# Two 128x1024 blocks transposed by DMA instead of by TensorE, and one load put behind them, in an adaLN transformer block

## The chip, the cores and the metric

The kernel runs on one core of a Trainium2 chip. The metric is the device time of one execution in microseconds (us); beside it stands the span, the time from the first to the last instruction in a profiled execution.

In the text, "chunk" is 128 tokens (2048 tokens make 16 chunks), PE is TensorE, DVE is VectorE, ACT is ScalarE, POOL is GpSimd, SP is the queue that issues all DMA. A PSUM bank is a buffer that PE writes its results to; it has to be emptied ("evacuated") by DVE or ACT before it is used again. The granted clock is the share of its full clock that PE was given. "Landing" is the time at which a transfer has arrived.

## The reference, cut to what matters

```python
mod = (silu(c) @ w_mod)            # six rows of 1024: sa, ca, ga, sb, cb, gb
h = layernorm(x) * (1 + ca) + sa   # x: 2048 x 1024
q, k, v = split(h @ wqkv)          # 32 heads
# linear attention: phi(k)^T v summed over all tokens, then phi(q) times it
x = x + ga * (attention(q, k, v) @ wo)
h = layernorm(x) * (1 + cb) + sb
x = x + gb * ((gelu(h @ w_gate) * (h @ w_up)) @ w_down)
```

## The kernel before

Every chunk passes through the same steps: LN statistics on DVE, the normalized chunk "xhat" (DVE, 128 tokens x 1024), a transpose into `H1` (features on partitions), the modulation `mod1` (DVE, multiply and add in place on `H1`), and then the k, v and q matmuls. There are two ways to transpose. `t1` uses PE (eight 128x128 transposes into a PSUM bank, copied out by ACT); `t1d` is one DMA. Chunks 0 to 5 use the first, chunks 6 to 15 the second.

```python
def t1(c_, tb):                       # by PE
    b_, rng = xh_buf(c_)
    for dc in range(NDC):             # NDC = 8
        sch.op(T, lambda e, dc=dc: e.transpose(PS16(tb, dc * P, (dc + 1) * P), b_[:, dc * P:(dc + 1) * P], IDENT[:, :]), ...)
    sch.op(A, lambda e: e.activation(H1[sg][:, :, ci * P:(ci + 1) * P], PS16(tb)..., ACTF.Copy), ...)

def t1d(c_, stream=Q):                # by DMA, issued from SP
    b_, rng = xh_buf(c_)              # three buffers in rotation
    tdma(stream, H1[sg][:, :, ci * P:(ci + 1) * P], b_[:, :], ...)
...
w_dma(WV, ...); w_dma(WV, ...)        # SP queue, in this order
x_dma(4, 8)
w_dma(WQ, ..., 0, 512)
w_dma(WQ, ..., 512, 1024)
x_dma(8, 12)                          # tokens 1024 to 1535, 2 KB per token
...
for c_ in range(4):
    ...                               # two v blocks of eight matmuls each
    if c_ == 0:
        ln1(4)
        for k, t in enumerate((4, 5, 10, 11)):
            wm_dma(t, k)              # four loads of 1 MB, modulation weights
    if c_ >= 1:
        kvacc(c_ - 1)                 # phi(k)^T v of one chunk
    if c_ == 1:
        ln1(5)
    if c_ == 2:
        ln1(6)
        x_dma(12, 16)
        t1d(6)
        t1(4, 4)
        mod1(4, 1)
t1(5, 4)
mod1(5, 1)
for c_ in range(4, NCH):              # q blocks, k, v, kvacc, and ln1/t1d of chunk c_ + 3
    ...
```

A helper records the operations of each engine in the order of the program and puts in the semaphore waits. Each engine is given its own list, in that order. So where `ln1(5)` stands in the text matters only against other operations of the same engines, DVE above all.

Near 175 to 200 us, after the loop, the last twelve q blocks run, and their PSUM banks rotate.

```python
b = (0, 1, 2, 0)[qn[0]] if qn[0] < 4 else (qn[0] + 1) % 2    # bank of the next q block
...
den(0, 3); rb_load(0); rb_load(1)     # den: denominators of attention (PE); their reciprocals stored, and loaded back broadcast, by DMA
kvbd()                                # DVE
q_next(); q_next()
for u in range(NG):                   # NG = 8
    q_next()
    if u == 0:
        kvt()                         # eight PE transposes, one ACT copy
    else:
        w2_pair(u - 1)                # "W2 products": wo times a transposed kv block
    ...                               # pq_scale needs the loaded reciprocals
```

Of the kernel before, what the change touches and what calls it, by code (L numbers as in the profile page):

```python
# [214 lines left out]
def bass_adaLN_cond__linear_attn_block__geglu_ffn__prompt_kernel(  # L215
# [15 lines left out]
    with ExitStack() as es:  # L231
# [79 lines left out]
        def r_sm(name):  # L311
            return [(SMO[name], SMO[name] + SMSZ[name], name)]
# [7 lines left out]
        def r_xs(c0, c1):  # L320
            return [(OFF_XALL + c0 * D * 2, OFF_XALL + c1 * D * 2, "xall")]
# [4 lines left out]
        def r_h1(sg, k0=0, k1=NDC, s0=0, s1=SGW):  # L326
            return r_t8(H1O[sg], f"h1T{sg}", k0, k1, s0, s1)
# [54 lines left out]
        def pr(b):  # L382
            return [(b * 2048, (b + 1) * 2048)]
# [4 lines left out]
        def PS16(b, c0=0, c1=1024):  # L388
            return ps16[:, b * 1024 + c0: b * 1024 + c1]
# [41 lines left out]
        def x_dma(c0, c1):  # L431
            return sch.dma(Q, lambda e: e.dma_start(XALL[:, c0:c1, :], x_v[:, c0:c1, :]), wr=r_xs(c0, c1), note=f"x{c0}")

        def wm_dma(t, sl):
            return sch.dma(Q, lambda e: e.dma_start(WMST[sl][:], wm_v[:, :, t * 512:(t + 1) * 512]), wr=r_wm(sl), note=f"wm{t}")

        def w_dma(dst, off, name, kind, c0, c1, dc0=0, dc1=NDC):
            return sch.dma(Q, lambda e: e.dma_start(dst[:, dc0:dc1, c0:c1], wqkv_v[:, dc0:dc1, kind * D + c0:kind * D + c1]),
                           wr=[t_ for dc in range(dc0, dc1) for t_ in r_w(off, name, dc, c0, c1)], note=f"{name}.{dc0}.{c0}")
# [21 lines left out]
        x_dma(4, 8)  # L461
        w_dma(WQ, OFF_WQ, "wq", 0, 0, 512)
        w_dma(WQ, OFF_WQ, "wq", 0, 512, 1024)
        x_dma(8, 12)


        sch.op(T, lambda e: e.transpose(PS16(4, 0, NDC), C8[:, :], IDENT[0:NDC, 0:NDC]),
# [10 lines left out]
        def ln_stats(c_, tag):  # L478
            src = XALL[:, c_, :]
            sch.op(V, lambda e: e.bn_stats(STA[:, c_, 0:6], src[:, 0:512]), rd=r_x(c_), wr=r_smc("st", c_, 48), note=f"bn1 {tag}{c_}")  # L480
            sch.op(V, lambda e: e.bn_stats(STA[:, c_, 6:12], src[:, 512:1024]), rd=r_x(c_), wr=r_smc("st", c_, 48), note=f"bn2 {tag}{c_}")
            sch.op(V, lambda e: e.bn_aggr(MVA[:, c_, :], STA[:, c_, :]), rd=r_smc("st", c_, 48), wr=r_smc("mv", c_, 8), note=f"aggr {tag}{c_}")
            sch.op(V, lambda e: e.tensor_scalar(VEA[:, c_:c_ + 1], MVA[:, c_, 1:2], 1e-5, None, op0=ALU.add),
                   rd=r_smc("mv", c_, 8), wr=r_smc("ve", c_, 4), note=f"ve {tag}{c_}")
            sch.op(G, lambda e: e.tensor_tensor(RSA[:, c_:c_ + 1], VEA[:, c_:c_ + 1], NEGHALF[:, :], ALU.pow),
                   rd=r_smc("ve", c_, 4) + r_sm("neghalf"), wr=r_smc("rs", c_, 4), deps=[last_g[0]], note=f"rstd {tag}{c_}")

        def ln_nm(c_):
            sch.op(V, lambda e: e.scalar_tensor_tensor(NMA[:, c_:c_ + 1], MVA[:, c_, 0:1], -1.0, RSA[:, c_:c_ + 1],
                                                       op0=ALU.mult, op1=ALU.mult),  # L490
                   rd=r_smc("mv", c_, 8) + r_smc("rs", c_, 4), wr=r_smc("nm", c_, 4), note=f"nm {c_}")

        def xhat_dve(c_, dst, rng):
            sch.op(V, lambda e: e.tensor_scalar(dst[:, :], XALL[:, c_, :], MVA[:, c_, 0:1], RSA[:, c_:c_ + 1],
                                                op0=ALU.subtract, op1=ALU.mult),
                   rd=r_x(c_) + r_smc("mv", c_, 8) + r_smc("rs", c_, 4), wr=rng, note=f"xhat {c_}")

        def xhat_act(c_, dst, rng):
            sch.op(A, lambda e: e.activation(dst[:, :], XALL[:, c_, :], ACTF.Identity, bias=NMA[:, c_:c_ + 1], scale=RSA[:, c_:c_ + 1]),
                   rd=r_x(c_) + r_smc("nm", c_, 4) + r_smc("rs", c_, 4), wr=rng, note=f"xhata {c_}")  # L500

        def xh_buf(c_):
            i = c_ % 3
            return XH[i], r_2k(XHO[i], f"xh{i}")

        def ln1(c_, eng="dve"):
            b_, rng = xh_buf(c_)
            ln_stats(c_, "A")
            if eng == "dve":
                xhat_dve(c_, b_, rng)  # L510
            else:
                ln_nm(c_)
                xhat_act(c_, b_, rng)

        def t1(c_, tb):
            b_, rng = xh_buf(c_)
            sg, ci = divmod(c_, CPG)
            for dc in range(NDC):
                sch.op(T, lambda e, dc=dc: e.transpose(PS16(tb, dc * P, (dc + 1) * P), b_[:, dc * P:(dc + 1) * P], IDENT[:, :]),  # L519
                       rd=rng + r_sm("ident"), pwr=pr(tb), note=f"T1 {c_}.{dc}")  # L520
            sch.op(A, lambda e: e.activation(H1[sg][:, :, ci * P:(ci + 1) * P], PS16(tb).rearrange("p (a b) -> p a b", a=NDC), ACTF.Copy),
                   prd=pr(tb), wr=r_h1(sg, 0, NDC, ci * P, (ci + 1) * P), note=f"h1raw {c_}")
# [3 lines left out]
        def tdma(stream, dst, src, rng, wr_, note):  # L526
            d_ = [last_t[0]] if last_t[0] is not None and last_t[0].stream != stream else []
            last_t[0] = sch.dma(stream, lambda e: e.dma_start_transpose(out=dst, in_=src), rd=rng, wr=wr_, deps=d_, note=note)

        def t1d(c_, stream=Q):  # L530
            b_, rng = xh_buf(c_)
            sg, ci = divmod(c_, CPG)
            tdma(stream, H1[sg][:, :, ci * P:(ci + 1) * P], b_[:, :], rng, r_h1(sg, 0, NDC, ci * P, (ci + 1) * P), f"T1 {c_}")
# [73 lines left out]
        def kv_mm(c_, kind, jg, bank, dcs):  # L607
            sg, ci = divmod(c_, CPG)
            W_, off, name = (WK, OFF_WK, "wk") if kind == "k" else (WV, OFF_WV, "wv")
            o = None  # L610
            for dc in dcs:
                o = sch.op(T, lambda e, dc=dc: e.matmul(PS(bank), H1[sg][:, dc, ci * P:(ci + 1) * P], W_[:, dc, jg * 512:(jg + 1) * 512],  # L612
                                                        start=(dc == 0), stop=(dc == NDC - 1)),
                           rd=r_h1(sg, dc, dc + 1, ci * P, (ci + 1) * P) + r_w(off, name, dc, jg * 512, (jg + 1) * 512),
                           pwr=(pr(bank) if dc == 0 else ()), note=f"{kind} c{c_} jg{jg} dc{dc}")
            if dcs[-1] == NDC - 1:
                pset_writer(bank, o)
# [5 lines left out]
        def v_evac(c_, jg, bank):  # L623
            i = c_ % 3
            sch.op(A, lambda e: e.activation(VS[i][:, jg * 4:jg * 4 + 4, 0:P], PS(bank).rearrange("p (a b) -> p a b", a=4), ACTF.Copy),
                   prd=pr(bank), wr=r_vs(i, jg * 4, jg * 4 + 4, 0, P), note=f"vcp{c_}.{jg}")

        def kvacc(c_):
            for g in range(NG):
                kb, koff = KVB[g]  # L630
                first = (c_ == 0 and g % 3 == 0)
                lastg = {5: 2, 6: 5, 7: 7}[kb]
                stop = (c_ == NCH - 1 and g == lastg)
                o = sch.op(T, lambda e, g=g, kb=kb, koff=koff, first=first, stop=stop: e.matmul(  # L634
                    PS(kb, koff, koff + V_W), PK[c_ % 5][:, g * P:(g + 1) * P], VS[c_ % 3][:, g, 0:V_W],
                    start=first, stop=stop, skip_group_check=True),
                    rd=r_pk(c_ % 5, g * P, (g + 1) * P) + r_vs(c_ % 3, g, g + 1, 0, V_W),
                    pwr=(pr(kb) if first else ()), note=f"kvacc c{c_} g{g}")
                if stop:
                    pset_writer(kb, o)  # L640
# [3 lines left out]
        def nb():  # L644
            b = bank_i[0] % 4
            bank_i[0] += 1
            return b
# [94 lines left out]
        for c_ in range(4):  # L742
            for jg in range(2):
                b = nb()
                kv_mm(c_, "v", jg, b, list(range(NDC)))
                v_evac(c_, jg, b)
            if c_ == 0:
                ln1(4)
                for k, t in enumerate((4, 5, 10, 11)):
                    wm_dma(t, k)  # L750
            if c_ >= 1:
                kvacc(c_ - 1)
            if c_ == 1:
                ln1(5)
            if c_ == 2:
                ln1(6)
                x_dma(12, 16)
                t1d(6)
                t1(4, 4)
                mod1(4, 1)  # L760
        t1(5, 4)
        mod1(5, 1)


# [385 lines left out]
```

## Time and profile before

| | before |
|---|---|
| time, median of 3 runs (range) | 843.18 us (842.88 to 844.29) |
| span of the profiled run | 841.3 us |
| PE busy | 830.7 us, 99% |
| granted PE clock | full in all 40 slices |
| one group of eight PE transposes, on PE | 0.45 us |

From the page of the kernel before, the head, the PE line of part 1 and the engines' shares of the chain of waits (part 4):

```profile
span 841.3 us, 11255 instructions
PE 830.7 (99%) x4149; PEld 387.9 (46%) x4229; DVE 492.0 (58%) x883; ACT 294.9 (35%) x483; POOL 24.4 (3%) x64
PE 96%; DVE 2%; issue 1%; ACT 1%; DMA 0%; ACTq 0%
```

PE is the bottleneck. Time can only be won by work taken off PE, or by gaps in it.

The timeline of PE in the stretch that the change touches. Columns: start, duration, engine, line and operation, output and inputs, form, count.

```profile
38.56 0.62 PE L634 MATMUL ps_all<-vs,pk 128*128 128x129 bf16 x8
39.01 3.62 PE L612 MATMUL ps_all<-wv,h1T 128*128 128x512 bf16 x16
42.47 0.62 PE L634 MATMUL ps_all<-vs,pk 128*128 128x129 bf16 x8
42.92 0.61 PE L519 MATMUL ps_all<-ident,xh 128*128 128x128 bf16 x8
43.37 3.62 PE L612 MATMUL ps_all<-wv,h1T 128*128 128x512 bf16 x15
46.82 0.62 PE L634 MATMUL ps_all<-vs,pk 128*128 128x129 bf16 x8
47.27 0.61 PE L519 MATMUL ps_all<-ident,xh 128*128 128x128 bf16 x8
47.72 3.62 PE L653 MATMUL ps_all<-h1T,wq 128*128 128x512 bf16 x16
```

A group overlaps with the next one, so the duration column is longer than its price. The price is the distance between starts: 43.37 - 42.92 = 0.45 us for the transposes of chunk 4 (L519), 47.72 - 47.27 = 0.45 us for those of chunk 5. There is no gap between the groups.

The timeline of the SP queue before (issue times, not transfer times):

```profile
26.69 5.58 SPq L438 DMA_DIRECT2D wq<-in_A_wqkv_dram  x2
32.32 3.75 SPq L432 DMA_DIRECT2D xall<-in_A_x_dram  x1
36.19 11.74 SPq L435 DMA_DIRECT2D wmst<-in_w_mod_dram  x4
47.98 3.15 SPq L432 DMA_DIRECT2D xall<-in_A_x_dram  x1
51.23 9.72 SPq L528 DMA_TRANSPOSE h1T<-xh  x2
```

The loads keep the DMA engines full (about 350 GB/s) until 57 us. The last x load landed 11.1 us after its issue, the DMA transpose of chunk 6 behind it 8.8 us after its issue, at 60.0; in an empty queue a transpose lands after 3.1 us.

The timeline of DVE before: xhat of chunks 4 and 5, and their modulations (eight instructions each). In brackets stands the idle time before, and what ended it.

```profile
40.20 0.55 DVE L494 TENSOR_SCALAR xh<-xall,mv,rs 128x1024 bf16<-128x1024 bf16 x1 [0.66 <-POOL rs L485]
43.17 0.55 DVE L494 TENSOR_SCALAR xh<-xall,mv,rs 128x1024 bf16<-128x1024 bf16 x1 [0.66 <-POOL rs L485]
46.60 1.87 DVE L538 TENSOR_SCALAR h1T<-h1T,modt 128x128 bf16<-128x128 bf16 x8
48.98 1.87 DVE L538 TENSOR_SCALAR h1T<-h1T,modt 128x128 bf16<-128x128 bf16 x8 [0.51 <-ACT h1T L521]
```

### The profile page before, as it was taken

The numbers are of one execution on the slowest core, as the hardware profiler recorded it, in microseconds if no ns is written. First come the engines' busy times: TensorE is split into PE (matmuls) and PEld (weight loads), VectorE is DVE, ScalarE is ACT, GpSimd is POOL, SyncE is SP. The second block draws the span as 40 slices with busy tenths as digits, with TensorE's granted clock in tenths as the row PEclk, the third lists the DMA queues.
The fourth block names the chain that finished last, engine by engine and source line by source line (L and its number), as shares of the span: only waits on it lengthen the run. The fifth ranks groups of instructions, "written<-read, shape, count | busy, mean of one in ns | idle before, by whom it ended". The sixth has DMA issues, their size and how long they took to land.

```text
span 841.3 us, 11255 instructions
## 1 busy us (share of the span) xinstructions
PE 830.7 (99%) x4149; PEld 387.9 (46%) x4229; DVE 492.0 (58%) x883; ACT 294.9 (35%) x483; POOL 24.4 (3%) x64
## 2 busy tenths in 40 slices
PE   8999999999999999999999999999999999999998
PEld 4454444444444444444444444444444444444445
DVE  5666767867785555654455665346666535655522
ACT  2343333335513344420355442044444104445300
POOL 2000000000200000010000001000000000000000
PEclk9999999999999999999999999999999999999999
DMA  9991824029778587340555533055553305555000
GB/s 286 354 285 26 263 47 105 14 54 233 165 165 252 155 253 206 105 97 23 149 153 154 153 102 69 26 157 150 150 151 101 75 19 158 152 157 141 7 19 26
DMA packets 181750, 112.70 MB, mean 134 GB/s; under 512 B 33080, under 2 KB 172728, under 8 KB 180672
## 3 DMA queue, kind: packets, MB, share of 16 engines
q1 hardware_dynamic: 181696, 111.98, 49.0%
q8 instruction: 34, 0.56, 0.3%
q14 instruction: 20, 0.16, 0.1%
HBM read 100.67 MB, written 4.47 MB: 125 GB/s over the span
## 4 chain that ended last, share of the span: by engine, by line
PE 96%; DVE 2%; issue 1%; ACT 1%; DMA 0%; ACTq 0%
PE ps_all L1006 23%; PE ps_all L1031 23%; PE ps_all L1003 22%; PE ps_all L612 12%; PE ps_all L934 7%; PE ps_all L653 6%; PE ps_all L668 1%; PE ps_all L634 1%; DVE h1T L538 1%; PE ps_all L584 0%; PE ps_all L836 0%; PE ps_all L565 0%; PE ps_all L519 0%; DVE ww L1019 0%; DVE ww L1016 0%
## 5 line engine op out<-in xcount | busy, mean ns | idle before, releaser
L1006 PE MATMUL ps_all<-h2T,wu 128*128 128x512 bf16 x896 | 339.6, 379 | 2.0
L1003 PE MATMUL ps_all<-h2T,wg 128*128 128x512 bf16 x859 | 325.6, 379 | 0.0
L1031 PE MATMUL ps_all<-wd,yT 128*128 128x512 bf16 (+1 forms) x907 | 193.2, 372 | 0.9
L1014 ACT ACTIVATE q<-ps_all 128x512 f32<-128x512 f32 x112 | 66.9, 597 | 229.4 <-PE ps_all L1003 224.5
L1031 PEld LDWEIGHTS ps_all<-wd,yT 128*128 128x128 bf16 x924 | 90.4, 98 | 103.2
L1003 PEld LDWEIGHTS ps_all<-h2T,wg 128*128 128x128 bf16 x896 | 87.7, 98 | 105.8 <-issue 0.2
L1006 PEld LDWEIGHTS ps_all<-h2T,wu 128*128 128x128 bf16 x896 | 87.7, 98 | 105.6
L1016 DVE SCALAR_TENSOR_TENSOR ww<-q,ps_all 128x512 f32<-128x512 f32 x112 | 77.0, 688 | 88.2 <-ACT guh L1015 88.2
L1019 DVE SCALAR_TENSOR_TENSOR ww<-th,guh 128x512 f32<-128x512 f32 x112 | 77.6, 693 | 77.9 <-ACT th L1018 77.9
L1018 ACT ACTIVATE th<-ww 128x512 f32<-128x512 f32 x112 | 70.5, 630 | 85.8 <-DVE ww L1016 85.8
L1021 DVE TENSOR_TENSOR yT<-ww,ps_all 128x512 bf16<-128x512 f32 x112 | 76.9, 687 | 3.8
L1036 DVE TENSOR_TENSOR ps_all<-ps_all,gbb 128x512 f32<-128x512 f32 (+1 forms) x33 | 22.5, 683 | 94.8 <-PE ps_all L1031 94.8
L1015 ACT ACTIVATE guh<-ps_all 128x512 f32<-128x512 f32 x112 | 66.3, 592 | 0.0
L601 ACT ACTIVATE eb<-ps_all 128x512 f32<-128x512 f32 x64 | 37.5, 601 | 77.9 <-PE ps_all L612 37.8
L653 PE MATMUL ps_all<-h1T,wq 128*128 128x512 bf16 x245 | 56.8, 379 | 1.4 <-DVE pq L604 0.7
L612 PE MATMUL ps_all<-wv,h1T 128*128 128x512 bf16 x254 | 57.8, 379 | 0.2
L612 PE MATMUL ps_all<-wk,h1T 128*128 128x512 bf16 x251 | 57.6, 379 | 0.2
L934 PE MATMUL ps_all<-w,pq 128*128 128x512 bf16 x251 | 56.0, 379 | 0.3
L602 DVE TENSOR_SCALAR eb<-eb 128x512 f32<-128x512 f32 x64 | 27.1, 424 | 34.0 <-ACT eb L601 33.6
L934 PEld LDWEIGHTS ps_all<-w,pq 128*128 128x128 bf16 x256 | 25.0, 98 | 30.2 <-issue 0.2
L612 PEld LDWEIGHTS ps_all<-wv,h1T 128*128 128x128 bf16 x256 | 24.9, 98 | 30.0 <-DVE eb L602 0.6
L612 PEld LDWEIGHTS ps_all<-wk,h1T 128*128 128x128 bf16 x256 | 24.6, 98 | 29.8 <-DVE h1T L538 1.5
(81 smaller groups left out, 398.8 us busy)
## 6 DMA issues: line engine op xcount, KB each, us to landing
wg<-in_B_w_gate_dram SPq DMA_DIRECT2D x56, 512.0 KB, 4.1
wu<-in_B_w_up_dram SPq DMA_DIRECT2D x56, 512.0 KB, 5.3
wmst<-in_w_mod_dram SPq DMA_DIRECT2D x8, 1024.0 KB, 11.6
rb<-scr_rd SPq DMA_DIRECT2D x32, 256.0 KB, 6.9
wd<-in_B_w_down_dram SPq DMA_DIRECT2D x7, 1024.0 KB, 7.6
wmq<-in_w_mod_dram SPq DMA_DIRECT2D x8, 512.0 KB, 7.0
out_dram<-xall SPq DMA_DIRECT2D x31, 128.0 KB, 1.7
xall<-in_A_x_dram SPq DMA_DIRECT2D x3, 1024.0 KB, 11.9
```

Source lines behind the costliest of these rows:

```text
L612: o = sch.op(T, lambda e, dc=dc: e.matmul(PS(bank), H1[sg][:, dc, ci * P:(ci + 1) * P], W_[:, dc, jg * 512:(jg + 1) * 512], start=(dc == 0 ...
L653: o = sch.op(T, lambda e, dc=dc: e.matmul(PS(b), WQ[:, dc, qc * P:(qc + 1) * P], H1[sg][:, dc, :], start=(dc == 0), stop=(dc == NDC - 1)), ...
L934: last[half] = sch.op(T, lambda e, g=g, half=half: e.matmul(PS(b0 + half), PQ[sg][:, g, ci * P:(ci + 1) * P], W2[:, g, half * 512:(half + ...
L1003: og = sch.op(T, lambda e, dc=dc: e.matmul(PS(bg), WG[slot][:, dc, e_ * P:(e_ + 1) * P], H2[sg][:, dc, :], start=(dc == 0), stop=(dc == ND ...
L1006: ou = sch.op(T, lambda e, dc=dc: e.matmul(PS(bu), WU[slot][:, dc, e_ * P:(e_ + 1) * P], H2[sg][:, dc, :], start=(dc == 0), stop=(dc == ND ...
L1014: sch.op(A, lambda e: e.activation(Q1[j][:, :], PS(bg), ACTF.Square, scale=math.sqrt(GELU_A)), prd=pr(bg), wr=rq, note=f"q1 {fc}")
L1015: ogh = sch.op(A, lambda e: e.activation(GUH[j][:, :], PS(bg), ACTF.Copy, scale=0.5), prd=pr(bg), wr=rg, note=f"gh {fc}")
L1016: sch.op(V, lambda e: e.scalar_tensor_tensor(WW[j][:, :], Q1[j][:, :], 1.0, PS(bg), op0=ALU.add, op1=ALU.mult), rd=rq, prd=pr(bg), wr=rw, ...
L1018: sch.op(A, lambda e: e.activation(TH[j][:, :], WW[j][:, :], ACTF.Tanh, scale=GELU_C), rd=rw, wr=rt, note=f"th {fc}")
L1019: sch.op(V, lambda e: e.scalar_tensor_tensor(WW[j][:, :], TH[j][:, :], 1.0, GUH[j][:, :], op0=ALU.add, op1=ALU.mult), rd=rt + rg, wr=rw, n ...
L1021: sch.op(V, lambda e: e.tensor_tensor(YT[:, fc, :], WW[j][:, :], PS(bu), ALU.mult), rd=rw, prd=pr(bu), wr=r_yt(fc), note=f"yT {fc}")
L1031: o = sch.op(T, lambda e, b=b, fc=fc, c0=c0, c1=c1, n=n: e.matmul(PS(b, 0, n), YT[:, fc, ci * P:(ci + 1) * P], WDT[fc // 4][:, fc % 4, c0:c1],
```

## The change

The intent: PE is full, DMA is not needed for latency here, so the transposes of chunks 4 and 5 go to DMA as well. Their DMA transposes must not stand behind 6 MB of loads; so they are recorded before the x load of tokens 1024 to 1535 and the modulation weights.

```diff
         w_dma(WQ, OFF_WQ, "wq", 0, 512, 1024)
-        x_dma(8, 12)
 ...
             if c_ == 0:
                 ln1(4)
+                t1d(4)
+                ln1(5)
+                t1d(5)
+                x_dma(8, 12)
                 for k, t in enumerate((4, 5, 10, 11)):
                     wm_dma(t, k)
             if c_ >= 1:
                 kvacc(c_ - 1)
-            if c_ == 1:
-                ln1(5)
             if c_ == 2:
                 ln1(6)
                 x_dma(12, 16)
                 t1d(6)
-                t1(4, 4)
                 mod1(4, 1)
-        t1(5, 4)
         mod1(5, 1)
```

## The prediction

> **What bounds the kernel.** TensorE. The page has PE busy 830.7 of 841.3 us, full granted clock, and a chain of waits that is 96% PE. The change touches the stretch from 37 to 68 us. There the timeline shows PE back to back: kvacc of chunk 1 at 42.47, eight 128x128 transposes of chunk 4 at 42.92, v matmuls at 43.37; kvacc of chunk 2 at 46.82, eight transposes of chunk 5 at 47.27, q matmuls at 47.72. There is no gap to close; only work can be taken off PE.
>
> **What goes.** 16 PE transposes. The chain lists each eight with 0.45 us (at 43.08 and 47.44): 0.90 us, all on the chain. (The Trainium skill, "VectorE: DVE Perf Modes", section "The three transpose paths", gives 390 ns on TensorE against 1309 ns by DMA for 128x128; pipelined, this trace shows 56 ns on PE.) Also two ACT evacuations of 1.02 us, at 43.57 and 47.92; ACT is a third busy there, so they are worth nothing.
>
> **What comes.** Two DMA transposes. In an empty queue SP takes 1.23 us to issue one and it lands after 3.1; the one behind the 1 MB loads took 4.27 and 8.8.
>
> **What moves.** The order on DVE does not change at all: LN of 4, 5, 6, then the modulations of 4 and 5. The SP queue does change: the x load of tokens 1024 to 1535 and, after it, four 1 MB modulation loads now stand behind transposes that wait for DVE. xhat 4 ends at 40.75, xhat 5 at 43.72. Before, the x load was issued at 32.3, the four from 36.2.
>
> Deadlines, from issue plus time to landing:
> - The wq halves land at 39 and 42; then the DMA queue is empty. Chunk 4's transpose should land at 44 to 45, chunk 5's at about 47. DVE modulates 4 at 46.6 and 5 at 48.5. No wait, or some tenths; before, the second waited 0.51 us for ACT.
> - DMA (about 350 GB/s before) starves from 42 to 45.5, so the end of the burst moves from 60 to about 63.5 (estimate from that gap). Chunk 6's DMA transpose lands near 64 (before 60.0), chunk 7's near 65 (62.8). They are needed at 66.5: a margin of 1.5 us, and DVE could be 2 us late before a PSUM bank came free late for PE.
> - The x load lands near 48.5, needed at 69. The modulation weights land by 61, needed at 80.
>
> **On the critical path:** minus 0.90 us, nothing added. Behind it PE is back to back, so the gain should survive: 843.2 - 0.9 = 842.3 us, 0.1%, about the spread of three runs (842.88 to 844.29).
>
> **What would show it.** PE: no transposes at 43 and 47, the first q matmuls at 46.8 in place of 47.7, every later stage 0.9 earlier (first den matmuls 178.5 to 177.6). DVE: modulation of chunk 4 without a DMA wait. DMA rate: a dip from 42 to 45 us, the burst ending 3 us later. SP queue: its longest new wait for xhat 4 (32.3 to 40.8).
>
> **What would make it wrong.** Transposes 4 or 5 landing after 50; 6 and 7 landing after 69, which would stall DVE and then PE; a DMA transpose slowing PE's operand reads. Each would eat the 0.9 us, hardly more than 2 us. Twice the gain would mean that PE paid more around the transposes than their own time.
>
> Chances: faster by over 2% 0.005, within 2% 0.985, slower by over 2% 0.01. Range 841.2 to 843.5.

## The result, and the profile after

| | before | changed |
|---|---|---|
| first comparison, median (range), 6 runs each | 843.33 (842.88 to 844.29) | 843.03 (842.07 to 844.63) |
| ratio of the fast runs, 95% interval | | 0.9995 (0.9982 to 1.0008) |
| span of the profiled run | 841.3 | 840.2 |
| first kvacc to first q block, in the trace | 9.16 | 8.27 |
| first kvacc to first output chunk, in the trace | 162.91 | 162.01 |
| first kvacc to the end of the span | 802.7 | 801.9 |

Ratios are computed as the mean time of one kernel's fast runs over that of the other's of the same rounds, so they are not quite the ratio of the medians quoted. By the clock alone the change is not clear of the noise. The trace shows it: counted from the first kvacc (38.56 us before, 38.28 after; the start of the kernel varies by some tenths from run to run), the first q block comes 0.89 us earlier, and 0.90 us is still there at the first output chunk at 200 us (before, then changed):

```profile
201.47 3.62 PE L934 MATMUL ps_all<-w,pq 128*128 128x512 bf16 x15
200.29 3.62 PE L933 MATMUL ps_all<-w,pq 128*128 128x512 bf16 x16
```

To the end of the span 0.8 us of it is left.

The page of the changed kernel, the same three lines:

```profile
span 840.2 us, 11305 instructions
PE 833.6 (99%) x4213; PEld 386.6 (46%) x4213; DVE 491.6 (59%) x883; ACT 292.7 (35%) x481; POOL 24.4 (3%) x64
PE 98%; DMA 1%; DVE 1%; SPq 0%; issue 0%
```

PE's busy time seems to rise although work was removed. That is the records: some matmul records are missing from a trace, and fewer are missing here (4213 against 4149, with 16 fewer instructions issued). Busy time can't be used for an effect of 1 us; distances between starts can.

The timeline of PE in the changed kernel:

```profile
38.28 0.62 PE L633 MATMUL ps_all<-vs,pk 128*128 128x129 bf16 x8
38.73 3.62 PE L611 MATMUL ps_all<-wv,h1T 128*128 128x512 bf16 x16
42.19 0.62 PE L633 MATMUL ps_all<-vs,pk 128*128 128x129 bf16 x8
42.64 3.62 PE L611 MATMUL ps_all<-wv,h1T 128*128 128x512 bf16 x16
46.09 0.62 PE L633 MATMUL ps_all<-vs,pk 128*128 128x129 bf16 x8
46.55 3.62 PE L652 MATMUL ps_all<-h1T,wq 128*128 128x512 bf16 x16
```

The two L519 groups are gone, and nothing came in their place. The prediction named a risk, that a DMA transpose slows PE's reading of its operands: the v matmuls that ran beside the two DMA transposes took 46.09 - 42.64 = 3.45 us from start to start, as in the kernel before (46.82 - 43.37). So there was no slowing. The SP queue of the changed kernel:

```profile
26.66 5.09 SPq L438 DMA_DIRECT2D wq<-in_A_wqkv_dram  x2
40.81 4.19 SPq L527 DMA_TRANSPOSE h1T<-xh  x2
45.05 0.58 SPq L432 DMA_DIRECT2D xall<-in_A_x_dram  x1
45.73 8.07 SPq L435 DMA_DIRECT2D wmst<-in_w_mod_dram  x4
53.84 2.91 SPq L432 DMA_DIRECT2D xall<-in_A_x_dram  x1
56.85 24.55 SPq L527 DMA_TRANSPOSE h1T<-xh  x4
```

SP stood for 9.0 us (31.8 to 40.8) waiting for xhat 4. The two transposes were issued at 40.8 and 43.8 and landed 3.2 and 2.7 us later, at 44.0 and 46.5. The DMA rate meanwhile fell to nothing (59 GB/s at 40 us, 0 at 41, 5 at 44) and was back at full only from 48. All later loads shifted: the last x load landed at 65.1 us in place of 59.1, and the burst ended at 66.4 in place of about 60 (the 66.4 includes the transpose of chunk 7; in the kernel before, that one came after the burst). The timeline of DVE shows what that costs there:

```profile
46.58 3.65 DVE L537 TENSOR_SCALAR h1T<-h1T,modt 128x128 bf16<-128x128 bf16 x16
66.93 2.14 DVE L537 TENSOR_SCALAR h1T<-h1T,modt 128x256 bf16<-128x256 bf16 x8 [0.61 <-DMA h1T<-xh]
```

The modulations of 4 and 5 run through without a wait. But those of chunks 6 and 7 now wait 0.61 us for the DMA transpose of chunk 7, which before had landed at 62.8, 4.6 us ahead of need (67.40). PE did not notice.

So two things are to be tested: that the gain is just the two groups' price, and that the moved load is harmless, and by how much.

### The profile page after: what moved, and what is told of

Its sections match the earlier page's. It is cut to its first block, busy times and chain, and to the rows that moved or that the text cites. A ratio compares the mean times of both kernels' runs of the same rounds, so it can differ in the third digit from the quotient of the medians.

```text
span 840.2 us, 11305 instructions
## 1 busy us (share of the span) xinstructions
PE 833.6 (99%) x4213; PEld 386.6 (46%) x4213; DVE 491.6 (59%) x883; ACT 292.7 (35%) x481; POOL 24.4 (3%) x64
## 4 chain that ended last, share of the span: by engine, by line
PE 98%; DMA 1%; DVE 1%; SPq 0%; issue 0%
PE ps_all L1030 23%; PE ps_all L1002 23%; PE ps_all L1005 23%; PE ps_all L611 13%; PE ps_all L933 7%; PE ps_all L652 6%; PE ps_all L633 1%; DMA xall<-in_A_x_dram 1%; PE ps_all L583 0%; PE ps_all L835 0%; PE ps_all L564 0%; PE ps_all L667 0%; PE ps_all L847 0%; PE ps_all L518 0%; DVE kvbd L822 0%
## 5 line engine op out<-in xcount | busy, mean ns | idle before, releaser
L1002 PE MATMUL ps_all<-h2T,wg 128*128 128x512 bf16 x896 | 339.6, 379 | 0.0
L652 PE MATMUL ps_all<-h1T,wq 128*128 128x512 bf16 x256 | 58.7, 379 | 0.7 <-DVE pq L603 0.7
```

Source lines behind the costliest of these rows:

```text
L652: o = sch.op(T, lambda e, dc=dc: e.matmul(PS(b), WQ[:, dc, qc * P:(qc + 1) * P], H1[sg][:, dc, :], start=(dc == 0), stop=(dc == NDC - 1)), ...
L1002: og = sch.op(T, lambda e, dc=dc: e.matmul(PS(bg), WG[slot][:, dc, e_ * P:(e_ + 1) * P], H2[sg][:, dc, :], start=(dc == 0), stop=(dc == ND ...
```

## The experiments

All kernels gave the reference's result. The theory (A): PE loses the price of two groups, 0.90 us, nothing else moves the time, and DVE has about 2 us of slack behind a late transpose before PE waits. Rivals: the moved load makes the gain or takes it back; PE paid more or less for a group than its own time.

### The changed kernel again

> The changed kernel once more, for the size of the time. Theory A (PE loses only the transposes' own time): 0.90 us less than before, about 842.4 beside 843.3. Rival B (the gain is given back later, or lies in noise of another cause): no difference. Both expect q matmuls of the first block 0.89 us nearer to the first kvacc than before (8.27 us in place of 9.16).

Measured: median 842.48 us (5 runs) beside 843.14 (9 runs of before), ratio 0.9994 (0.998 to 1.0007); first kvacc to first q block 46.41 - 38.15 = 8.26 us; span 840.1; DVE waited 1.02 us for chunk 7's transpose. The trace repeats to 0.01 us. The time still doesn't leave the noise. All 11 runs of the changed kernel average 842.99, all 35 runs of before 843.45. Counted from the first kvacc, the span ends after 801.95 us (before 802.74, changed 801.92).

### Only the load moved

Against the kernel before:

```diff
-        x_dma(8, 12)
 ...
                 ln1(4)
+                ln1(5)
+                x_dma(8, 12, deps=[sch.streams[V][-1]])   # waits for xhat 5
 ...                                                       # t1(4, 4) and t1(5, 4) stay
```

> Only the move of the x load (behind xhat 5); chunks 4 and 5 are still transposed on PE. Theory A: the loads are not on the critical path, so the time is that of before (843.3, within 0.3) and the first q matmuls start 9.16 us after the first kvacc, as before; the burst of loads ends some 3 to 5 us later than before (60), and DVE may wait up to 0.6 us for chunk 7's transpose. Rival C (the gain comes from moving the load out of the way): about 0.9 us less than before.

Measured: median 843.28 beside 843.14, ratio 0.9997 (0.9985 to 1.001); first kvacc to first q block 47.63 - 38.47 = 9.16 us, as before; span 841.2.

```profile
38.47 0.62 PE L633 MATMUL ps_all<-vs,pk 128*128 128x129 bf16 x8
47.63 3.62 PE L652 MATMUL ps_all<-h1T,wq 128*128 128x512 bf16 x16
```

The load's move alone wins nothing and loses nothing. Rival C falls. DVE did not wait for chunk 7 at all here; the burst ended a little above 65.

### The DMA transposes, the load left in front of them

Against the changed kernel:

```diff
         w_dma(WQ, OFF_WQ, "wq", 0, 512, 1024)
+        x_dma(8, 12)
 ...
                 t1d(5)
-                x_dma(8, 12)
```

> The DMA transposes without the move of the x load: it stays ahead of them in the SP queue and lands near 44.7. Theory A: the transposes of chunks 4 and 5 land near 46 and 48, before or at the time DVE needs them (46.6 and 48.5); PE as in the changed kernel, 0.9 us less than before; the burst ends earlier than in the changed kernel (64 in place of 66.5). Rival D (the move of the load is what makes the DMA transposes possible): DVE waits 1 us or more for chunk 4, and PE gives back part of the 0.9.

Measured: median 842.37 beside 843.14, ratio 0.9989 (0.9976 to 1.0003); first kvacc to first q block 46.43 - 38.16 = 8.27; span 840.1.

```profile
38.16 0.62 PE L634 MATMUL ps_all<-vs,pk 128*128 128x129 bf16 x8
46.43 3.62 PE L653 MATMUL ps_all<-h1T,wq 128*128 128x512 bf16 x16
```

There was no DVE wait for a transpose, and the burst ended at 64 us. Chunk 4's transpose landed at 44.9 (4.2 us after its issue). The whole gain is there without the move of the load. Rival D falls.

### The same again, as a base for later runs

> The version with the DMA transposes and the x load ahead of them, again, as the base of the next three. Theory A: 0.9 us below before, span near 840.1, no wait of DVE for a DMA transpose up to 90 us.

Measured: median 842.52 beside 843.33, ratio 0.9994 (0.9981 to 1.0006); span 840.7 with a start that was 0.6 us later (first kvacc 38.78); to the first q block 8.26. This time chunk 4's transpose took 6.0 us, to 47.1, and DVE waited 0.2 us for it. So the load in front does cost margin at chunk 4, and the load behind costs margin at chunk 7 (0.61 and 1.02 us of waiting in two traces). Both stay inside the slack. The ten runs of this version average 842.54 us, 0.91 below the 35 of before. That this is so close to 0.90 is partly luck: the average of before contains runs of 845.28 and 846.91; the medians (842.38 and 843.21) differ by 0.83.

### Each group of PE transposes eleven times

Against the kernel before:

```diff
-            for dc in range(NDC):
+            for dc in list(range(NDC)) * copies:
 ...
-                t1(4, 4)
+                t1(4, 4, 11)
 ...
-        t1(5, 4)
+        t1(5, 4, 11)
```

> The kernel before, with each of the two groups of eight PE transposes issued eleven times in place of once (the result is the same): the price of one group, twenty times over. Theory A: one group costs 8 x 56 ns = 0.45 us, so 20 more cost 9.0 us: about 852.3. Rival E (PE pays also for what stands around a group: a switch, a wait for the bank): a group's own price is below 0.45, so less than 9.0 us here while one group's removal gained 0.45. If 219 ns, the record's length, were the price, it would be 35 us.

Measured: median 851.88 beside 843.14, ratio 1.0102 (1.0088 to 1.0116): 8.74 us for 20 groups more, 0.44 us for one. The timeline of PE in this kernel:

```profile
42.70 5.08 PE L519 MATMUL ps_all<-ident,xh 128*128 128x128 bf16 x88
47.62 3.62 PE L612 MATMUL ps_all<-wv,h1T 128*128 128x512 bf16 x16
```

47.62 - 42.70 = 4.92 us for 88 transposes, 55.9 ns each, and 0.45 us for eight. This settles the price: two groups are worth 0.87 us by the clock, without a profile (the interval of the ratio allows 0.74 to 0.98), and 0.90 us by the trace. One group costs as much per transpose as eleven in a row, so nothing is seen to be paid at a group's edges. The Trainium skill, "TensorE: Matmul & The Clock Gate", Part 1, gives 55.6 ns from start to start for matmuls of 128 columns at full clock; this trace agrees for transposes, with its 55.9.

### The DMA transposes behind all loads

Against the kernel before:

```diff
                 x_dma(12, 16)
                 t1d(6)
-                t1(4, 4)
+                t1d(4)
                 mod1(4, 1)
-        t1(5, 4)
+        t1d(5)
         mod1(5, 1)
```

> The DMA transposes of chunks 4 and 5 at the place where the PE transposes stood: in the SP queue behind the x loads, the four 1 MB modulation loads and the transpose of chunk 6. Theory A with its deadlines: they land near 61 to 63 in place of 44 and 47, DVE starts to modulate chunk 4 near 61.5, PE stands still from about 50 to 62, the kernel takes about 11 us (9 to 14) more than before, 854. Rival F (a DMA transpose does not queue behind loads issued before it): they land by 55 and PE loses less than 5 us.

Measured: median 855.99 (2 runs) beside 843.21, ratio 1.0145 (1.012 to 1.0171). DVE waited 11.87 us for chunk 4's transpose, until 61.75. In the timeline of PE:

```profile
62.12 6.41 PE L612 MATMUL ps_all<-wk,h1T 128*128 128x512 bf16 x16 [8.74 <-DVE h1T L538]
68.36 3.62 PE L612 MATMUL ps_all<-wv,h1T 128*128 128x512 bf16 x16
```

The deadline was real, and a DMA transpose does wait behind the loads issued before it; rival F falls. (The Trainium skill, "DMA: Bandwidth & Descriptors", section "Queues, rings and completion order", says that each DMA engine consumes the descriptors of a ring in order; the trace agrees: the last load landed at 59.7, the transposes of chunks 4 and 5 at 61.7 and 62.7.) So the place of the transposes in the queue is a necessary part of the change, even though the x load's place is not.

One thing was not expected. The 16 k matmuls behind the wait took 68.36 - 62.12 = 6.24 us, where the same 16 take 3.45 elsewhere. PE's granted clock was 0.50 from 58 to 66 us. Not all of this was lost: the DVE operation that frees the bank for the v matmuls (pq) ended only at 66.5, so at full clock they could have started some 1.9 us earlier, not 2.8 (an estimate from these times). The run with 2 MB more, below, shows the clock again. (This profiled run also had a slow start, with PE waiting 1.35 us for a load near 21 us and the clock at 0.50 for 3.4 us soon after it; it reached the first kvacc 2.9 us later than before. Of the 13.9 us of span, 2.9 are that start, 11.7 the stretch shown, less 0.9 for the transposes saved.)

### The burst made longer by 1 MB and by 2 MB

To see where DVE's lateness begins to cost, unused loads of 1 MB were put in front of the modulation weights. They make the transposes of chunks 6 and 7 later. Against the changed kernel (the helper's check that forbids overwriting unread data is switched off, not shown):

```diff
                 x_dma(8, 12)
+                for sg_ in (3,):          # (3, 2) for 2 MB
+                    sch.dma(Q, lambda e, sg_=sg_: e.dma_start(H1[sg_]..., x_v[:, 0:4, :]), wr=r_h1(sg_), ...)
```

> The changed kernel with one more 1 MB load (its data is not used) ahead of the modulation loads: the burst ends 2.9 us later, chunk 7's transpose lands near 69.8, DVE waits some 3.5 us for it. Theory A (DVE has about 2 us to spare before PE notices, counted from 66.5): PE loses 0 to 1 us against the changed kernel. Rival G (no slack: each us of DVE lateness costs PE one): 2.9 us more.

> As the last, with two 1 MB loads: the burst ends 5.8 us later, chunk 7's transpose lands near 72.7. Theory A: the k matmuls of chunk 6 (PE ready for them at 71.6) wait over 1 us and a PSUM bank comes free late behind the modulation and LN of DVE: PE loses 2 to 4.5 us against the changed kernel. Rival H (plenty of slack): below 0.5 us.

Measured, with the changed kernel for comparison (time in the trace is counted from the first kvacc to the first output chunk):

| | changed | 1 MB more | 2 MB more |
|---|---|---|---|
| DVE waits for chunk 7's transpose | 0.61 | 3.93 | 7.69 |
| first kvacc to first output chunk | 162.01 | 163.41 | 167.17 |
| lost against the changed kernel | | 1.40 | 5.16 |
| time, median | 843.03, 842.48 | 843.96 | 847.75 |
| ratio to before | 0.9995, 0.9994 | 1.0009 (0.9989 to 1.0028) | 1.0048 (1.0029 to 1.0067) |

With 1 MB more, DVE's modulation of chunks 6 and 7 and then PE:

```profile
70.24 2.14 DVE L537 TENSOR_SCALAR h1T<-h1T,modt 128x256 bf16<-128x256 bf16 x8 [3.93 <-DMA h1T<-xh]
76.46 3.63 PE L611 MATMUL ps_all<-wv,h1T 128*128 128x512 bf16 x16 [1.23 <-DVE pq L603]
```

PE waited for a PSUM bank that DVE freed late (by the record 1.23 us; from start to start the loss is 1.40). So DVE's slack is 3.93 - 1.40 = 2.5 us, counted from the time when DVE was ready for the modulation. Rival G (no slack) falls; the theory's 2 us was somewhat short, and the loss lies above its 0 to 1 us. With 2 MB more:

```profile
74.30 2.14 DVE L537 TENSOR_SCALAR h1T<-h1T,modt 128x256 bf16<-128x256 bf16 x8 [7.69 <-DMA h1T<-xh]
74.70 5.47 PE L611 MATMUL ps_all<-wk,h1T 128*128 128x512 bf16 x16 [2.61 <-DVE h1T L537]
80.53 1.69 PE L611 MATMUL ps_all<-wv,h1T 128*128 128x512 bf16 x7 [0.35 <-DVE pq L603]
```

Now the modulation itself came too late for the k matmuls. The loss, 5.16 us, is above the 2 to 4.5 that was expected; rival H falls. Against the undisturbed course (the q block at 68.47 plus 3.45) the k matmuls start 74.70 - 71.92 = 2.78 us late, and the v matmuls behind them follow after 5.83 us in place of 3.45, that is 2.38 us more; of these the duration column has 5.47 - 3.62 = 1.85, the rest is the second wait. The stretch-by-stretch view of this kernel shows why the k matmuls were slow. Columns: stretch, its length, busy time of PE, PEld (PE's weight loads), DVE, ACT and POOL with counts, granted PE clock, DMA share, GB/s.

```profile
74.00:76.00 2.00, 1.30 (x6) 0.50 (x6) 1.70 (x7) 0.00 (x0) 0.00 (x0) 0.98 0.00 0
76.00:78.00 2.00, 2.00 (x6) 0.73 (x6) 1.93 (x5) 0.46 (x1) 0.00 (x0) 0.50 0.00 0
78.00:80.00 2.00, 2.00 (x7) 0.64 (x5) 1.27 (x5) 0.14 (x1) 0.55 (x1) 0.66 0.00 0
```

After the gap of 2.6 us PE's clock went to half for about 3.4 us (from 80 us on it was full again), and the records of the k matmuls grew from 379 to 632 ns. After the gap of 1.2 us in the other kernel the clock stayed at 1.00. The Trainium skill, "TensorE: Matmul & The Clock Gate", Part 1, describes this halving after idleness, with a window of about 3.4 us that is free-running; its table at the end asks for no gaps above about 3 us. Here 2.6 us was enough once, and in the run with all transposes late (its slow start) a wait of 1.35 us between thin matmuls of one column was also followed by 3.4 us at half clock. So these runs give no firm limit.

The halved clock did not make the loss larger, though. The v matmuls had to wait for DVE's bank in any case: they start 80.53 - 74.30 = 6.23 us after the modulation here, and 76.46 - 70.24 = 6.22 us after it in the run with 1 MB more, at full clock. And the four runs with 2 MB more took 847.39 to 847.81 us with a mean clock of 0.998, and 847.82 with 1.000. So lateness is free up to 2.5 us and costs one for one above it: 3.93 - 1.40 and 7.69 - 5.16 both leave 2.53.

### The same move once more: the kv transposes by DMA

> The changed kernel with the same move once more: the eight transposes of the kv blocks (0.45 us of PE at 183.5) go to DMA as well, ahead of the loads of the reciprocals; the last q blocks also rotate through five PSUM banks in place of two, which takes away PE's 0.66 us wait for DVE at 184.7, and the W2 products follow one block later. Theory A: transpose lands near 185.7, first W2 product at about 187.5 does not wait; 0.45 + 0.66 = 1.1 us less than the changed kernel in the span, 2.0 less than before: about 841.3. Rival I (DVE's backlog binds there, so that the wait only moves): 0 to 0.5 us.

Against the changed kernel:

```diff
-            for g in range(NG):
-                sch.op(T, ... e.transpose(PS16(4, g * P, (g + 1) * P), KVBD[:, g, :], IDENT[:, :]), ...)
-            sch.op(A, ... KVT <- PS16(4) ...)
+            tdma(Q, KVT[:, :, :], KVBD[:].rearrange("p a b -> p (a b)"), r_kvbd(0, NG), R_KVT, "kvT")
 ...
-            b = (0, 1, 2, 0)[qn[0]] if qn[0] < 4 else (qn[0] + 1) % 2
+            b = (0, 1, 2, 0, 1, 5, 6, 7, 0, 1, 5, 6)[qn[0]]
 ...                                  # kvbd and kvt ahead of the rb loads; w2_pair one block later,
                                      # two of them after the last block
```

Measured: median 844.13 beside 843.21, ratio 1.0007 (0.9992 to 1.0022), where 2.0 us less than before had been expected. Counted from the first kvacc, its span ends 1.3 us later than the changed kernel's (803.2 against 801.9). The trace shows two waits of PE that were made by the new order: 1.23 us for ACT (the two W2 products at the end share their banks) and 1.02 us for DVE (the first output chunk needs a bank that the last q block now used). A bad test of the idea, so the parts were taken singly, on the version with the load in front as the base. The diffs of the next three are against that base.

### Only the banks

```diff
-            b = (0, 1, 2, 0)[qn[0]] if qn[0] < 4 else (qn[0] + 1) % 2
+            b = (0, 1, 2, 0, 1, 6, 7, 0, 1, 6, 0, 1)[qn[0]]
```

> That base with only another rotation of PSUM banks for the last q blocks (two more banks, free by then; the last blocks avoid those that the first output chunk needs). PE's 0.66 us wait for DVE near 184.7 should go, and the gain stay: span 0.6 to 0.7 below the base, 839.5. If DVE's backlog binds anyway, the wait comes back at a later block: 0 to 0.2.

Measured: median 841.70 (841.12 to 842.00) beside 843.33, ratio 0.9983 (0.997 to 0.9995). First kvacc to first output chunk 161.17, against 162.00 of the base: 0.83 us. The timelines of PE, of the base and of this kernel:

```profile
183.97 0.61 PE L828 MATMUL ps_all<-ident,kvbd 128*128 128x128 bf16 x8
185.23 1.90 PE L653 MATMUL ps_all<-h1T,wq 128*128 128x512 bf16 x8 [0.65 <-DVE pq L604]
```

```profile
184.28 0.61 PE L828 MATMUL ps_all<-ident,kvbd 128*128 128x128 bf16 x8
184.72 1.89 PE L653 MATMUL ps_all<-h1T,wq 128*128 128x512 bf16 x8
```

From start to start the distance falls from 1.26 to 0.44 us. The span of the profiled run, 840.2, was expected at 839.5; it includes a start that was 0.3 us later than the base's (first kvacc 39.09).

### Only the kv transposes

```diff
 ...                                  # kvt by DMA, kvbd and kvt ahead of the rb loads, banks as they were
```

> That base with the eight kv transposes (0.45 us of PE) by DMA, banks as they were. They stand just before PE's wait for a bank that DVE frees (0.66 us, until 184.7), so PE should arrive 0.45 earlier and wait 1.1: no gain from the move, span within 0.2 of the base. Rival (taking work off PE always pays): 0.45 less.

Measured: median 842.40, ratio 0.9993 (0.998 to 1.0005), no different from the base (0.9994); the median of the base was 842.52. The timeline of PE:

```profile
184.55 1.90 PE L653 MATMUL ps_all<-h1T,wq 128*128 128x512 bf16 x8 [1.10 <-DVE pq L604]
```

Counted from the first kvacc, this block starts at 184.55 - 38.09 = 146.46; in the base at 185.23 - 38.78 = 146.45. PE was freed of 0.45 us of work and waited 0.45 us longer. (Later q blocks lose 0.26 us against the base, so that the first output chunk starts after 162.26 us in place of 162.00.) The same eight transposes, at the same price, were worth their full time at 43 us and nothing here.

### Both

```diff
+            b = (0, 1, 2, 0, 1, 6, 7, 0, 1, 6, 0, 1)[qn[0]]
+            for g in {2: (0,), 3: (1, 2), 4: (3,), 5: (4,), 6: (5,), 7: (6,)}.get(u, ()):
+                w2_pair(g, 2 + 2 * (g % 2))
 ...                                  # pq_scale(0, 0) one block later
```

> Both: the kv transposes by DMA and the wait for the bank taken away by the rotation, with the W2 products spread so that no two groups share banks at the end, and the scaling of pq one block later (the loads it needs come 1 us later). Expected 0.45 + 0.66 = 1.1 us below the base, span 839.0, some 2.0 us below before. In the earlier try of this PE waited 1.23 for ACT and 1.02 for DVE at the end; both should be gone.

Measured: median 842.32, ratio 0.9989 (0.9976 to 1.0003), span 840.1. To the first output chunk it takes 199.57 - 38.84 = 160.73, 1.27 us less than the base and 0.44 less than the banks alone: here the kv transposes' price was won. But some is given back later, and at the end of the span, counted from the first kvacc, this kernel is only 0.66 us ahead of the base (801.26 against 801.92), the banks alone 0.81 (801.11). So the expected 1.1 us was missed. At 253 us PE waits 0.39 us for DVE, and DVE had waited 0.95 and 1.54 us (before 242.81 and 247.97) for a load of the reciprocals, against one such wait of 1.05 us with the banks alone. Why these later loads came late was not tried. Its time is not clear of the banks alone, whose median is lower; that stays the best version, 1.63 us below before.

## Why the prediction was right

- **The size and its cause: right.** 0.90 us was taken from the chain; the trace gives 0.89 and 0.90, the elevenfold groups 0.44 us each by the clock. The predicted 842.3 us stands beside medians of 843.03 and 842.48, inside the range 841.2 to 843.5. That says little by itself: the range also holds 843.33, the median of before, and the runs of before spread from 842.4 to 846.9. What shows the gain is the trace and the elevenfold groups.
- **DVE order, deadlines of chunks 4 and 5: right.** Predicted landings 44 to 45 and about 47; measured 44.0 and 46.5, no wait.
- **The end of the burst: mis-sized.** Predicted 63.5 from a gap of 3.5 us; measured 66.4. The loads started again at 45.05, about as predicted (45.5), but DMA was starved from 40, not from 42, and full again only from 48. I took the time when the wq halves landed (42) from a trace in which the x load followed them in the queue; without it the rate fell from 39 us on, although the last of wq landed at 41.3. With only the load moved, it was issued 1.2 us earlier (43.84) and the burst ended 1.2 us earlier (65.2): the end follows the time of that issue. So chunk 6's transpose landed at 66.0 in place of 64, chunk 7's at 66.9 in place of 65; the margin of 1.5 us was gone, and DVE waited 0.61.
- **The slack of DVE: right enough.** 2 us predicted, 2.5 measured, and the first thing to come late for PE was a PSUM bank, as predicted. It is what kept the last point free of cost.
- **"Hardly more than 2 us" for a failure: too small.** A late transpose can cost far more: beyond the slack each us costs one, 5.2 us with 2 MB more in the queue and nearly 11 us with the transposes behind all loads (of these some 1.9 by the halved clock, an estimate).
- **What I did not see:** the move of the x load was not needed for the gain. It shifts margin from chunk 7 to chunk 4.

What is left open: the slower runs among the fast ones, 844.63 and 844.64 us of the changed kernel, 845.28 and 846.91 of before. Each of these four has a mean granted clock of 0.998, where the others have 1.000 (a few 0.999). One stretch of 3.4 us at half clock, as seen above, would give that mean and cost at most 1.7 us (an estimate from that trace), about what the least late of them lost and less than the others did (1.6 to 3.7 us above the medians); no trace of those runs was taken.

## What to carry to other kernels

Where one engine is full, work taken off it is worth its start-to-start time, not its duration in the records, and only if no wait follows at once that absorbs it: the same eight transposes gave 0.45 us in one place and nothing in another, until the wait behind them was removed. A DMA that replaces compute work gets a deadline, so place it in the queue ahead of bulk loads, and count what the loads behind it will then miss. Effects of 0.1% are settled by distances between starts in the trace and by multiplying the cost, here elevenfold, not by repeating the same comparison.

## What the Trainium skill lacked or had wrong

- "TensorE: Matmul & The Clock Gate", the table "Why this matters for your kernels": it puts the limit for a PE gap at about 3 us. Here a gap of 2.6 us was followed by about 3.4 us at half clock (16 matmuls took 1.85 us longer, which cost the kernel nothing, because PE would have waited for DVE), and so was a wait of 1.35 us between matmuls of one column; a gap of 1.2 us was not.
- The same page, Part 4 (PE-mode transpose): it gives 390 ns alone and about 275 ns in one kernel's context for a 128x128 transpose, and says that full clock doesn't engage for transposes. Here the record of one transpose is 219 ns long. In a stream behind matmuls they took 55.9 ns each from start to start, 88 in a row over 4.9 us, at a granted clock of 1.00.
- "VectorE: DVE Perf Modes", "The three transpose paths": 1309 ns for one 128x128 by DMA. That section has no figure for a DMA of eight such tiles (other pages have general DMA figures, which were not tried here): here 2.7 to 3.2 us from issue to landing in an empty queue, 4.2 to 6.0 behind one 1 MB load still in flight, 8.8 to 9.2 behind a full queue.
